# A fused attention and low-rank mixer kernel: the mixer of batches 2 to 8 in strips of 32 columns and rows, and a first batch in another order

## The chip, the cores and the metric

One core of a Trainium2 chip runs the whole kernel. The metric is the device time of one execution in microseconds, as the median of repeated runs; the results also hold one profiled execution with its trace. The engines are TensorE (PE, matmuls; PEld is its weight load), VectorE (DVE), ScalarE (ACT), GpSimd (POOL) and SyncE (SP, which issues most transfers).

## The reference

Eight batches of attention with normed queries and keys, 12 heads, 448 tokens, head size 64; the result goes through a low-rank mixer over tokens and a two-layer network over channels.

```python
def _attn_ref(q, k, v, g_q, g_k):
    def rmsnorm(x, g):
        rms = np.sqrt(np.mean(x * x, axis=-1, keepdims=True) + 1e-06)
        return x / rms * g
    q_n, k_n = (rmsnorm(q, g_q), rmsnorm(k, g_k))
    scores = scale * np.matmul(q_n, k_n.transpose(0, 1, 3, 2))
    ...
    return np.matmul(attn, v)          # softmax of the scores

def _moe_ref(x, U, V, w_ch1, w_ch2):   # x: (8, 448, 768), rank of U and V: 32
    xt = x.transpose(0, 2, 1)
    h = xt @ U @ V
    u = x + h.transpose(0, 2, 1)
    ch = np.maximum(u @ w_ch1, 0.0) @ w_ch2
    return u + ch
```

## The kernel before

The order of the work on every engine is written out by hand. In the code the eight batches are numbered 0 to 7, so that batches 2 to 8 of the title are `b` = 1 to 7. Each batch has 12 heads in six pairs and three groups of four heads; a group's q, k and v are loaded together (`load`), squared (`squares`), summed on VectorE (`sums`), turned into inverse roots on ScalarE (`roots`, lines 165 to 171), scaled (`scale`, line 173) and transposed (`turn`, then `take_q` and `take_k`, lines 349 to 373; from group 6 on by transfers, `turn_dma`). `values` copies v on GpSimd.

For a pair, scores go to PSUM and through the exponential on ScalarE into `E`: in batches 0 and 1 by rows of 128 keys (`Sc`, line 403), later as a whole pair (`Spair`, line 421), of which each takes the two double-bank score buffers of the pool `ps_sc`. `V` (line 450) multiplies `E` with the values, one half of the tokens at a time, and VectorE divides into `x`.

The mixer of one batch follows when `x` is complete. For `b` >= 1: `mix_t` (line 480) forms x^T U for six blocks of 128 channels, 24 matmuls with blocks of x as weights and 32 columns of U moving. VectorE casts the result (line 487), `mix_tr` (line 491) turns it in two transposes, and `mix_rows` (line 530) multiplies it with `Vm`, a copy of V that has zeros outside 32 rows for each of four positions: 24 matmuls of 128 columns in eight pieces. VectorE adds x (line 546), and SP issues four transposing transfers into `uT` (line 552). Batch 0 uses `mix_t0`, `mix` and `mix_rows` with `tz` instead.

The network is `up` (line 554, six matmuls of 448 columns for each of 24 blocks, ReLU on ScalarE mostly) and `down` (line 598, parts of six matmuls of 384 columns, four parts to an output half). A list `mlp` holds these pieces, and the mixer of batch b + 1 is put among the `down` parts of batch b (`pre`, `PRE`, lines 770 to 795). A list `att` holds the attention of the later batches. The loop from line 884 on interleaves both by costs in microseconds and by a model of how far each engine is (`at`, `runs`, `ready`): a `Spair` isn't put directly behind a mixer piece, and loads are held back (`later`, `turning`) while a mixer's transposes are queued on SP.

The first batch has no network beside it. Its order stands in the dict `extra` (line 651), whose entry `(i, r)` is put behind the scores of row block r of pair i, and in the lines from 799 on. `keep_busy` runs matmuls of the identity whose result nobody reads. GpSimd also issues the loads of the two weight matrices (`weights`: four pieces of `w1b`, eight of `w2b`).

Of the kernel before, what the change touches and what calls it, by code (L numbers as in the profile page):

```python
# [9 lines left out]
FP32 = mybir.dt.float32  # L10
# [16 lines left out]
def kernel(  # L27
# [19 lines left out]
    P = 128  # L47
# [199 lines left out]
    for va, vl in zip(va_bufs, vl_bufs):  # L247
        nc.vector.memset(va[:, :, D:D1], 1.0)
        nc.vector.memset(vl, 0.0)
        for e in range(2):  # L250
            nc.vector.memset(vl[e * R:(e + 1) * R, :, e * D1 + D:(e + 1) * D1], 1.0)
    for t, eng in zip(kT_bufs, (nc.vector, nc.gpsimd)):
        eng.memset(t[D:P, :, SM:S], 0.0)
        eng.memset(t[0:D, :, S:], 0.0)
# [54 lines left out]
    Vm = consts.tile([P, NQ, S + R], BF16)  # L309

    nc.gpsimd.memset(Vm, 0.0)

    def prep_v(lo, hi):
        for m in range(lo, hi):
            r = slice(m * rank, (m + 1) * rank)
            cols = Vf[r].rearrange("r (p j) -> r j p", j=NT)
            nc.gpsimd.tensor_copy(Vm[r, m, :SM].rearrange("r (t i p) -> r i t p", i=2, t=NJ),
                                  cols[:, :2 * NJ].rearrange("r (i t) p -> r i t p", i=2))
            nc.gpsimd.tensor_copy(Vm[r, m, SM:S], cols[:, 2 * NJ])
# [9 lines left out]
    tb_bufs = [consts.tile([P, 2 * P], BF16, name=f"tb{i}") for i in range(2)]  # L329
# [150 lines left out]
    def mix_t(b):  # L480

        pt = ps.tile([P, KD, rank], FP32, name="pu", tag="ps")
        for dt in range(KD):
            for j in range(NW):
                nc.tensor.matmul(pt[:, dt, :], xs[b][:, j, dt * P:(dt + 1) * P], Ub[:, j if j < NJ else NJ + b % 2, :],  # L485
                                 start=(j == 0), stop=(j == NW - 1))
        nc.vector.tensor_copy(tb_bufs[b % 2][:, :KD * rank], pt.rearrange("p k r -> p (k r)"))
        runs("pe", 0.62)
        runs("dve", 0.35)

    def mix_tr(b):
        pt = ps.tile([P, 2, P], BF16, name="pw", tag="ps")
        for i in range(2):
            nc.tensor.transpose(pt[:, i, :], tb_bufs[b % 2][:, i * P:(i + 1) * P], ident)
        tTs[b] = headp.tile([P, 2, P], BF16, name="tT", tag="tT")
        nc.vector.tensor_copy(tTs[b], pt)
        runs("pe", 0.11)
        runs("dve", 0.3)
# [11 lines left out]
    def mix(b, dt, scalar=False):  # L510
# [3 lines left out]
        nc.tensor.matmul(ph, tz[:, dt * P:(dt + 1) * P], Vm[:, 0, :S], start=True, stop=False)  # L514
# [15 lines left out]
    def mix_rows(b, w, half):  # L530

        odd = b % 2
        off = 0 if odd else 64
# [3 lines left out]
        if b < ROWS_FROM:  # L537
            nc.tensor.matmul(ph, Vm[:, 0, vc:vc + P], tz[:, h], start=True, stop=True)
        for i in range(HALF // P) if b >= ROWS_FROM else ():
            dt = half * (HALF // P) + i  # L540
            nc.tensor.matmul(ph[:, i * P:(i + 1) * P], Vm[:, dt % NQ, vc:vc + P], tTs[b][:, dt // NQ, :],  # L541
                             start=True, stop=True)
# [6 lines left out]
        if half == 1 and b >= ROWS_FROM:  # L549
            full = xs[b][:, w, :] if w < NJ else u_rest[lo:hi, :]  # L550
            c = off + w * P
            nc.sync.dma_start_transpose(uT[:, :, c:c + hi - lo], full)
# [95 lines left out]
    def turns(gi):  # L648
# [9 lines left out]
        (1, 2): [(0.4, turn, (1, 0)), (0, take_q, (1, 0)), (0, take_q, (1, 1)), (0, keep_busy, (8,))],  # L658
# [4 lines left out]
        (2, 3): [V2(1, 1), (0, prep_u, ())],  # L663
        (3, 0): [(0, keep_busy, (6,))],
        (3, 1): [V2(2, 0)],
        (3, 2): turns(2),
        (3, 3): [V2(2, 1), (0, take_k, (2, 1)), (0, squares, (3, 0, pool)), (0, values, (2,)), (0, load, (5,)),
                 (0, weights, (1,)), (0, prep_v, (0, 1)), (0, squares, (3, 1, pool)), (0, weights, (1,))],
        (4, 0): [V2(3, 0)],
        (4, 1): [V2(3, 1), (0, sums, (3, 0))],  # L670
        (5, 0): [(0.9, mix_t0, (0, 512))],
        (5, 1): [V2(4, 0)],
        (5, 2): [V2(4, 1), (0.39, mix, (0, 0))],
        (5, 3): [(0.39, mix, (0, 1)), (0.2, mix_t0, (512, 640)), (0, prep_v, (1, NQ)), (0, weights, (2,))],
# [95 lines left out]
    PRE = (14, 20)  # L770
    mlp = []
    for b in range(B):
# [8 lines left out]
        if ROWS_FROM <= nb < B:  # L781
            pre[n - PRE[nb > 1]] = [(0.77, mix_t, (nb,), nb)]
            pre[n - PRE[nb > 1] + 1] = [(0.11, mix_tr, (nb,), nb)]
            for piece in range(2 * NW):
                pre.setdefault(n - PRE[nb > 1] + 2 + (piece if nb > 1 else piece // 2), []).append(
                    (0.17, mix_rows, (nb, *divmod(piece, 2)), nb))
# [27 lines left out]
    for part in PARTS:  # L814
        scale_part(1, *part, nc.vector)
# [136 lines left out]
```

## Time and profile before

| | us |
|---|---|
| median of 3 runs (lowest, highest) | 582.67 (581.82, 583.47) |
| the profiled execution | 582.16 |
| its span | 580.3 |
| TensorE busy in the span | 570.9 |
| ScalarE, GpSimd, VectorE busy | 308.2, 210.2, 196.3 |

The span is that of the recorded instructions; the time has some 1.9 us around it. Busy time of TensorE counts a matmul to its modelled end, and neighbours overlap, so what a matmul costs is read from the distance between starts. The granted TensorE clock is 1.00 throughout. In a timeline a row gives start, duration, engine, line, operation, tiles and count, and in brackets how long the engine had been idle and what ended that.

### The profile page before, as it was taken

Reading aid. Unit: us, or ns where it says so; the run is one execution under the profiler, and the core shown is the slowest. Engines: PE = TensorE matmul, PEld = TensorE weight load, DVE = VectorE, ACT = ScalarE, POOL = GpSimd, SP = SyncE. Lnnn points to the kernel's source line nnn. Section 1 sums busy time; section 2 is a strip of 40 time slices with the busy share of each in tenths; the row PEclk is TensorE's granted clock in tenths of the full one; section 3 lists DMA queues with packets and bytes.
Section 4 is the critical chain, followed back from the end, with each engine's and each line's share of the span. In section 5 each row is a group of like instructions: output and inputs, shape, how many; then the busy total and the mean of one; then the engine's idle time right before and its main releaser. Section 6 shows DMA issues by size and latency. Waiting matters only on the chain.

```text
span 580.3 us, 11778 instructions
## 1 busy us (share of the span) xinstructions
PE 570.9 (98%) x4850; PEld 338.7 (58%) x4850; DVE 196.3 (34%) x459; ACT 308.2 (53%) x510; POOL 210.2 (36%) x310
## 2 busy tenths in 40 slices
PE   8899999999999999999999999999999999999997
PEld 7655556555665556655566555665556555655565
DVE  5676656212353232521244230542034210410011
ACT  6866660787445776277635568357752444014300
POOL 5995684265314514334514532441531000000000
PEclk9999999999999999999999999999999999999999
DMA  9899999683547642765247745366204210330022
GB/s 235 168 241 241 244 232 223 128 209 73 135 79 170 156 106 35 175 179 130 36 123 116 179 104 122 80 159 150 36 16 102 49 28 1 54 76 1 1 55 55
DMA packets 104829, 68.21 MB, mean 118 GB/s; under 512 B 66632, under 2 KB 101704, under 8 KB 104776
## 3 DMA queue, kind: packets, MB, share of 16 engines
q1 hardware_dynamic: 95124, 57.83, 43.2%
q0 software_dynamic: 9408, 9.44, 9.7%
q8 instruction: 38, 0.62, 0.5%
q10 hardware_dynamic: 244, 0.20, 0.1%
q14 instruction: 15, 0.12, 0.1%
HBM read 52.20 MB, written 11.01 MB: 109 GB/s over the span
## 4 chain that ended last, share of the span: by engine, by line
PE 92%; ACT 2%; DMA 1%; POOL 1%; DVE 1%; issue 1%; SPq 0%; POOLq 0%; ACTq 0%
PE ph L558 36%; PE po L605 36%; PE pv L466 6%; PE sc L436 2%; PE pv L462 2%; PE sl L427 2%; PE sl L438 2%; PE pm L541 2%; PE po L592 1%; ACT E L416 1%; PE sc L415 1%; DMA qT<-qn 1%; PE pu L485 1%; DMA qf<-in_q_dram 1%; PE pt L354 1%
## 5 line engine op out<-in xcount | busy, mean ns | idle before, releaser
L605 PE MATMUL po<-w2b,hT 128*128 128x384 bf16 x1296 | 229.6, 326 | 0.0
L558 PE MATMUL ph<-uT,w1b 128*128 128x448 bf16 x1140 | 228.7, 352 | 0.0
L605 PEld LDWEIGHTS <-hT 128*128 128x128 bf16 x1296 | 122.1, 98 | 71.8
L558 PEld LDWEIGHTS <-w1b 128*128 128x128 bf16 x1140 | 108.3, 98 | 93.7 <-issue 0.7
L565 ACT ACTIVATE hT<-ph 128x448 bf16<-128x448 f32 x184 | 98.2, 551 | 116.6 <-PE ph L558 115.2
L429 ACT ACTIVATE E<-sl,gg 128x448 bf16<-128x448 f32 x72 | 41.6, 630 | 71.7 <-PE sl L427 71.7
L193 POOL TENSOR_TENSOR qn<-qf,rs 128x384 bf16<-128x384 f32 x36 | 29.9, 830 | 137.5 <-ACT rs L170 126.8
L386 POOL TENSOR_SCALAR qT<-qT,gg 128x448 bf16<-128x448 bf16 x36 | 50.5, 1403 | 73.6 <-DMA qT<-qn 63.5
L469 DVE RECIPROCAL r<-pv 128x4 f32<-128x4 f32 x96 | 17.5, 182 | 173.0 <-PE pv L466 172.8
L441 ACT ACTIVATE E<-sc,gg 128x896 bf16<-128x896 f32 x72 | 69.0, 1024 | 0.0
L615 DVE TENSOR_TENSOR ob<-po,x 128x384 f32<-128x384 f32 x46 | 25.7, 558 | 99.8 <-PE po L605 97.6
L466 PE MATMUL pv<-va,E 128*128 128x65 bf16 x1152 | 57.1, 194 | 0.0
L466 PEld LDWEIGHTS <-E 128*128 128x128 bf16 x1152 | 50.5, 98 | 6.3
L162 DVE TENSOR_REDUCE ssq<-sq 128x14 f32<-128x896 f32 x45 | 46.8, 1078 | 2.4 <-ACT sq L140 2.3
L462 PE MATMUL pv<-vl,E 128*128 128x130 bf16 x192 | 42.2, 220 | 0.3 <-ACT E L416 0.2
L470 DVE TENSOR_TENSOR x<-pv,r 128x256 bf16<-128x256 f32 x96 | 40.7, 424 | 3.3
L416 ACT ACTIVATE E<-sc,gg 128x896 bf16<-128x896 f32 (+1 forms) x42 | 37.5, 951 | 3.5 <-PE sc L415 3.3
L546 DVE TENSOR_TENSOR x<-pm,x 128x384 bf16<-128x384 f32 x48 | 26.1, 552 | 11.3 <-PE pm L541 9.1
L193 POOL TENSOR_TENSOR kp<-kf,rs 128x384 bf16<-128x384 f32 x36 | 29.9, 830 | 0.0
L169 ACT ACTIVATE rs<-ssq,eps 128x28 f32<-128x28 f32 (+1 forms) x25 | 7.9, 314 | 38.0 <-DVE ssq L162 33.7
L462 PEld LDWEIGHTS <-E 128*128 128x128 bf16 x192 | 18.7, 97 | 9.7 <-issue 2.0
L439 ACT ACTIVATE E<-sl,gg 128x448 bf16<-128x448 f32 x36 | 23.0, 638 | 0.0
(105 smaller groups left out, 401.0 us busy)
## 6 DMA issues: line engine op xcount, KB each, us to landing
qf<-in_q_dram SPq DMA_DIRECT2D x23, 448.0 KB, 3.8
kf<-in_k_dram SPq DMA_DIRECT2D x23, 448.0 KB, 5.3
vf<-in_v_dram SPq DMA_DIRECT2D x48, 192.0 KB, 5.3
out_dram<-ob SPq DMA_DIRECT2D x48, 192.0 KB, 2.8
w1b<-in_moe_w_ch_dram POOLq DMA_DIRECT2D x4, 1152.0 KB, 19.8
w2b<-in_moe_w_ch_dram POOLq DMA_DIRECT2D x8, 576.0 KB, 18.0
vf<-in_v_dram SPq DMA_DIRECT2D x48, 32.0 KB, 5.1
out_dram<-ob SPq DMA_DIRECT2D x13, 96.0 KB, 3.4
```

The costliest lines, as they stand in the source:

```text
L162: nc.vector.tensor_reduce(ssqs[gi][:, i, :], sqs.pop((gi, i)), AX, ALU.add)
L193: nc.gpsimd.tensor_tensor(main.rearrange("p (t i) d -> p i t d", i=2), src[:, c, :2 * NJ].rearrange("p (i t) d -> p i t d", i=2), rs[:, c, ...
L386: nc.gpsimd.tensor_scalar(qT[:, a], qT[:, a], gg[:, 0:1], None, ALU.mult)
L416: nc.scalar.activation(es[(b, pr)][:, 2 * r:2 * r + n, :], sc[:, :n, :S], AF.Exp, scale=scal, bias=bias)
L429: nc.scalar.activation(E[:, 4 + i, :], ts[i], AF.Exp, scale=scal, bias=bias)
L441: nc.scalar.activation(E[:, 2 * r:2 * r + 2, :], tiles[r][:, :, :S], AF.Exp, scale=scal, bias=bias)
L462: nc.tensor.matmul(pv[:, i].rearrange("p e d -> p (e d)"), E[:, 2 * NJ, w:w + P], vl[:, lp, :], start=True, stop=False)
L466: nc.tensor.matmul(pv[:, i, e, :], E[:, 2 * j + e, w:w + P], va[:, (first_h + step * e) * NJ + j, :], start=False, stop=(e == 1 and j == N ...
L470: nc.vector.tensor_tensor(xs[b].rearrange("p i (h d) -> p i h d", d=D)[:, 2 * half:2 * half + 2, h0:h0 + step + 1:step, :], pv[:, :, :, :D ...
L558: nc.tensor.matmul(ph, w1b[:, dt, ht * P:(ht + 1) * P], uT[:, dt, off:off + S], start=(dt == 0), stop=(dt == KD - 1))
L565: nc.scalar.activation(hT[:, ht, off:off + S], ph, AF.Relu)
L605: nc.tensor.matmul(po, hT[:, ht, col:col + P], w2b[:, ht, half * HALF:(half + 1) * HALF], start=(ht == 0), stop=(ht == KH - 1))
```

## The change

Mixer, `b` >= 1. `mix_t` now has U as weights, 32 columns of them, and 192 columns of x moving; four such strips g = 0 to 3 write to PSUM partitions 32g to 32g + 31, so that the result comes out with 32 ranks times four channel quarters on the partitions and is cast once. There are 16 matmuls. `mix_tr` and its copy are gone. `mix_two` takes two row blocks w at once: for each, four matmuls with 32 rows of `Vr` (V copied four times down the partitions, without zeros) as weights and 32 rows of the cast as moving data, 192 columns each, into four banks: both buffers of `ps_sc`. The additions and the transposes into `uT` stand in `mix_two`. In `mlp` it stands at `PRE` + 2 and + `GAP`. Before a `mix_two` the planner takes one `down` of the batch before while its model of ScalarE or VectorE is behind TensorE.

First batch. The squares of group 1's q go from ScalarE to GpSimd and those of group 2's k from GpSimd to ScalarE, those of group 1's k behind the first exponential; `scales(2)` moves from behind (2, 1) to behind (2, 0), `values(1)` from (1, 3) to behind these scales; `V2(0, 1)`, the turns of group 2, `V2(2, 0)` and the mixer of batch 0 get other places; `gg` is copied between the two parts of the key's scaling. `keep_busy(10)` goes and another takes 8 instead of 14. The constants of the third value buffer and the second key buffer, which VectorE and GpSimd filled at the start, are filled by GpSimd later (`fill_mixer`); the fills of `Vm` and `tb` go, and `prep_v` is one pass instead of four.

```diff
-    Vm = consts.tile([P, NQ, S + R], BF16)
-    nc.gpsimd.memset(Vm, 0.0)
+    Vr = consts.tile([P, S + R], BF16)
+    nc.vector.memset(Vr[:, S:], 0.0)
...
     def fill_mixer():
         nc.gpsimd.memset(Uz, 0.0)
-        for t in tb_bufs:
-            nc.gpsimd.memset(t, 0.0)
+        fill_values(2, nc.gpsimd)
+        fill_keys(1, nc.gpsimd)
...
-        pt = ps.tile([P, KD, rank], FP32, name="pu", tag="ps")
-        for dt in range(KD):
-            for j in range(NW):
-                nc.tensor.matmul(pt[:, dt, :], xs[b][:, j, dt * P:(dt + 1) * P], Ub[:, j if j < NJ else NJ + b % 2, :],
-                                 start=(j == 0), stop=(j == NW - 1))
-        nc.vector.tensor_copy(tb_bufs[b % 2][:, :KD * rank], pt.rearrange("p k r -> p (k r)"))
+        pt = ps.tile([P, QC], FP32, name="pu", tag="ps")
+        for j in range(NW):
+            for g in range(NQ):
+                nc.tensor.matmul(pt[g * rank:(g + 1) * rank, :], Ub[:, j if j < NJ else NJ + b % 2, :],
+                                 xs[b][:, j, g * QC:(g + 1) * QC], start=(j == 0), stop=(j == NW - 1))
+        tTs[b] = headp.tile([P, QC], BF16, name="tT", tag="tT")
+        nc.vector.tensor_copy(tTs[b], pt)
...
-    def mix_tr(b):
...
+    def mix_two(b, ws):
+        odd = b % 2
+        off = 0 if odd else 64
+        ts = [ps_sc.tile([P, 2, 512], FP32, name="sc", tag="sc") for _ in range(2)]
+        for i, w in enumerate(ws):
+            vc = w * P if w < NJ else (SM if odd else S - P)
+            for g in range(NQ):
+                r = slice(g * rank, (g + 1) * rank)
+                nc.tensor.matmul(ts[g // 2][:, g % 2, i * QC:(i + 1) * QC], Vr[r, vc:vc + P], tTs[b][r], start=True, stop=True)
+        runs("pe", 0.4)
+        for i, w in enumerate(ws):
...
+                nc.vector.tensor_tensor(full[:, h].rearrange("p (g c) -> p g c", g=2),
+                                        ts[half][lo:hi, :, i * QC:(i + 1) * QC],
+                                        xs[b][lo:hi, w, h].rearrange("p (g c) -> p g c", g=2), ALU.add)
+                runs("dve", 0.56)
+            c = off + w * P
+            nc.sync.dma_start_transpose(uT[:, :, c:c + hi - lo], full)
...
-        (0, 0): [(0, keep_busy, (8,))],
+        (0, 0): [(0, squares, (1, 1)), (0, take_k, (0, 1)), (0, sums, (1, 1)), (0, sums, (2, 0)), (0, keep_busy, (8,))],
...
-        (0, 2): scales(1) + [(0, squares, (2, 1, pool)), (0, keep_busy, (8,))],
+        (0, 2): scales(1) + [(0, weights, (1,)), (0, keep_busy, (8,))],
...
-        (1, 1): [V2(0, 0), (0, keep_busy, (6,))],
...
-        (1, 3): [(0.4, turn, (1, 1)), (0, take_k, (1, 0)), V2(0, 1), (0, take_k, (1, 1)), (0, sums, (2, 1)),
-                 (0, values, (1,)), (0, load, (4,)), (0, weights, (1,))],
-        (2, 1): scales(2) + [(0, weights, (1,)), V2(1, 0)],
+        (1, 1): [(0, squares, (2, 1)), V2(0, 0), (0, keep_busy, (6,))],
...
+        (1, 3): [(0.4, turn, (1, 1)), (0, take_k, (1, 0)), (0, sums, (2, 1)), (0, take_k, (1, 1)), (0, keep_busy, (4,))],
+        (2, 0): scales(2) + [(0, values, (1,)), (0, load, (4,)), (0, weights, (1,))],
+        (2, 1): [V2(1, 0)],
...
-        (3, 1): [V2(2, 0)],
-        (3, 2): turns(2),
...
+        (3, 1): [(0.4, turn, (2, 0)), (0, take_q, (2, 0)), (0, take_q, (2, 1))],
+        (3, 2): [(0.4, turn, (2, 1)), (0, take_k, (2, 0)), V2(2, 0)],
...
-        (5, 0): [(0.9, mix_t0, (0, 512))],
+        (5, 0): [(0, sums, (3, 0)), (0.45, mix_t0, (0, 256))],
...
+            at_ = n - PRE[nb > 1]
+            pre[at_] = [(0.6, mix_t, (nb,), nb)]
+            pre[at_ + 2] = [(0.4, mix_two, (nb, (0, 1)), nb)]
+            pre[at_ + GAP[nb > 1]] = [(0.4, mix_two, (nb, (2, 3)), nb)]
...
-    keep_busy(10)
-    for part in PARTS:
-        scale_part(1, *part, nc.vector)
+    scale_part(1, *PARTS[0], nc.vector)
     nc.vector.tensor_copy(gg, pg)
-    squares(1, 0)
+    scale_part(1, *PARTS[1], nc.vector)
     fill_mixer()
+    squares(1, 0, nc.gpsimd)
+    turn(0, 0)
+    keep_busy(8)
+    take_q(0, 0, True)
+    take_q(0, 1, True)
+    turn(0, 1)
+    keep_busy(14)
+    take_k(0, 0)
+    sums(1, 0)
...
+            if after_pair and mixes(f) or f is mix_two and max(at["act"], at["dve"]) > at["pe"]:
+                e = next((i for i in range(im, len(mlp)) if mlp[i][1] is down), None)
+                if e is not None and mlp[e][3] < mlp[im][3]:
+                    mlp.insert(im, mlp.pop(e))
```

Of batch 0's mixer only the places change: `mix_t0` of the first 512 channels is split in two and `mix(0, 0)` moves behind the last scores. The rest of the diff removes `squares(1, 1)`, `sums` and `take_k(0, 1)` from where they stood ahead of the loop, since they are in `extra` now, and adapts line by line to the new names.

More of the change, by code (lines that the diff above doesn't have):

```diff
@@ L513, in mix @@
         xb = xs[b][:, :, dt * P:(dt + 1) * P]
-        nc.tensor.matmul(ph, tz[:, dt * P:(dt + 1) * P], Vm[:, 0, :S], start=True, stop=False)
+        nc.tensor.matmul(ph, tz[:, dt * P:(dt + 1) * P], Vr[:, :S], start=True, stop=False)
         for j in range(NJ):
@@ L536, in mix_rows @@
         vc = w * P if w < NJ else (SM if odd else S - P)
[L537 to L542, printed above, removed]
+        nc.tensor.matmul(ph, Vr[:, vc:vc + P], tz[:, h], start=True, stop=True)
         x = xs[b][:, w, h]
@@ L548, in mix_rows @@
         runs("dve", 0.56)
[L549 to L552, printed above, removed]
     def up(b, ht):
@@ L821 @@
     values(0)
-    turn(0, 0)
-    keep_busy(14)
-    take_q(0, 0, True)
-    take_q(0, 1, True)
-    squares(1, 1)
-    turn(0, 1)
-    take_k(0, 0)
-    sums(1, 0)
-    sums(1, 1)
-    take_k(0, 1)
-    sums(2, 0)
     stage_tiles(3)
@@ L865, in mixes @@
     def mixes(f):
-        return f in (mix_t, mix_tr, mix_rows)
+        return f in (mix_t, mix_two)
     def ready(f, a):
@@ L875, in ready @@
         if f is sums and a[0] > DMA_FROM:
-            return not any(m[1] in (mix_t, mix_tr) for m in mlp[max(0, im - 1):im + 3])
+            return not any(m[1] is mix_t for m in mlp[max(0, im - 1):im + 3])
         if ca >= a_one:
@@ L918 @@
             f(*a)
-            turning = f is mix_t and a[0] > 0 or turning and a != (a[0], NW - 1, 1)
+            turning = f is mix_t or turning and not (f is mix_two and a[1][1] == NW - 1)
             cm += c
```

76 lines of the change are left out of this document (32 added, 44 removed).

## The prediction

> **What bounds the kernel now.** I read the page first, then the stretches by engine, then two engines' timelines. The first line is engine busy time; the digits are the busy tenths of 40 equal slices; the last two are stretches: busy time of each engine, granted clock, DMA share, GB/s.
>
> ```profile
> PE 570.9 (98%) x4850; PEld 338.7 (58%) x4850; DVE 196.3 (34%) x459; ACT 308.2 (53%) x510; POOL 210.2 (36%) x310
> ...
> PE   8899999999999999999999999999999999999997
> ...
> 0.00:41.00 41.00, 35.41 (x473) 26.55 (x474) 27.45 (x85) 30.48 (x47) 33.65 (x51) 1.00 0.95 213
> 41.00:580.00 539.00, 535.45 (x4379) 312.11 (x4377) 168.90 (x375) 277.69 (x464) 176.54 (x260) 1.00 0.50 110
> ```
>
> From 41 us to the end TensorE is the bound: it stands still for 3.6 of 539 us. There only less TensorE time counts, and any new wait of TensorE counts in full. Before 41 us TensorE partly runs filler (`keep_busy`), and ScalarE's exponentials of batch 0 set the pace. So I split the time into the head, to the last exponential of batch 0 at 35.5 us, and the chain of TensorE work behind it: a shift of the head moves the end by as much.
>
> The mixer of one batch on TensorE (start, duration, shape, count; an instruction's step is the next start minus its own, since durations overlap):
>
> ```profile
> 92.32 0.75 PE L485 MATMUL pu<-Ub,x 128*128 128x32 bf16 x24
> 92.92 1.14 PE L605 MATMUL po<-w2b,hT 128*128 128x384 bf16 x6
> 93.89 0.28 PE L494 MATMUL pw<-ident,tb 128*128 128x128 bf16 x2
> 94.01 1.14 PE L605 MATMUL po<-w2b,hT 128*128 128x384 bf16 x6
> 94.98 0.50 PE L541 MATMUL pm<-tT,Vm 128*128 128x128 bf16 x6
> 95.32 1.14 PE L605 MATMUL po<-w2b,hT 128*128 128x384 bf16 x6
> ...
> 106.16 0.36 PE L427 MATMUL sl<-qT,kT 64*128 64x448 bf16 x2
> 106.36 0.54 PE L436 MATMUL sc<-qT,kT 64*128 64x448 bf16 x4
> 106.83 0.36 PE L438 MATMUL sl<-qT,kT 128*128 128x448 bf16 x1
> ```
>
> `mix_t` steps 92.92 - 92.32 = 0.60, `mix_tr` 0.12, six `pm` 0.34, so 24 of them 1.36: 2.08 us a batch. The last lines show part-array matmuls, 64 rows each: two of 448 columns step 0.20 together, as long as one full-array one (six `ph` of 448 take 1.14, 0.19 each). So two row halves run side by side. Four step 0.47, two rounds of 0.187 plus 0.10: going into or out of the part-array form costs about 0.095 each way (the same on entry: 24 `po` of 0.1625 from 102.17 end at 106.07, `sl` starts at 106.16).
>
> The head, ScalarE and GpSimd:
>
> ```profile
> 12.10 2.80 ACT L416 ACTIVATE E<-sc,gg 128x896 bf16<-128x896 f32 x3
> 14.78 0.33 ACT L169 ACTIVATE rs<-ssq,eps 128x28 f32<-128x28 f32 x1
> ...
> 20.37 1.91 ACT L416 ACTIVATE E<-sc,gg 128x896 bf16<-128x896 f32 x2 [1.04 <-PE sc L415]
> 22.53 0.32 ACT L169 ACTIVATE rs<-ssq,eps 128x28 f32<-128x28 f32 x1 [0.26 <-DVE ssq L162]
> ...
> 28.27 4.33 ACT L416 ACTIVATE E<-sc,gg 128x896 bf16<-128x896 f32 x5 [0.21 <-PE sc L415]
> ```
>
> ```profile
> 12.13 1.68 POOL L143 TENSOR_TENSOR uT<-qf 128x896 f32<-128x896 f32 x1 [2.15 <-DMA qf<-in_q_dram]
> ...
> 20.41 0.82 POOL L201 CAST va<-vf 128x768 bf16<-128x768 f32 x1
> ...
> 23.25 1.68 POOL L174 TENSOR_TENSOR qn<-qf,rs 128x896 bf16<-128x896 f32 x1 [0.43 <-issue]
> ```
>
> ScalarE runs from 12.10 to 35.50 with only some 2 us of waits, most of it the 1.04 before group 1's first scores.
>
> **The mixer, seven times.** New `mix_t`: 16 matmuls of 192 columns, in four rounds of four column strips. A full-array matmul of 192 columns would step 0.083 (between `pm`, 0.34/6 = 0.057 at 128, and `po`, 0.1625 at 384). No row shows column strips, nor four parts at once. Bounds: side by side, 4 x 0.083 + 0.19 for entry and exit = 0.52; one after another, 16 x 0.083 + 0.19 = 1.52. I take the first, since the nearest row, the 64-row pair, is wholly side by side. `mix_tr` is gone. New `mix_two`: two rounds of four 32-row strips, 2 x 0.083 + 0.19 = 0.36, twice: 0.71 (one after another, 0.85 each). Sum 1.23 against 2.08: 0.85 x 7 = **-5.9 us**.
>
> VectorE gets the same 16 halves of additions over 384 columns (0.55 each), one 192-column cast as before (0.36), and loses a 0.29 copy; it is off the path. The four uT transposes per batch stay on SP's queue; the second pair now lies behind fewer `down` parts. The tightest case is the step into batch 3, where six parts and two V halves, 6.7 us, remain between the last `mix_two` and the first `up`. The additions take 2.2, two transposes queue at 1.25 each, the last lands 2.5 after issue: about 5.7. Hidden, with 1 us to spare; if two output issues (0.6 each) stand ahead, nothing is left.
>
> **A new wait.** `mix_two` takes both double-bank score buffers that `Spair` uses. TensorE must wait there for the exponentials, and all `down` matmuls behind it wait too. From the start of a `Spair` to its last exponential, rows of batch 4 give 3.9 us (305.91 to 309.79). In the new order three of the 14 `mix_two` stand 0.87 + 3 x 0.975 = 3.8 us behind it and the rest more; a modelled delay of ScalarE is ahead of that. In turn a `Spair` stands two `down` parts behind a `mix_two` once, 2.5 us until its first use against four additions and a latency, 2.8. Together 4 x 0.1 to 0.2: **+0.5**; bounds 0 and 3 (squares of 1.9 us on ScalarE in front of one `Spair` in two).
>
> **The head.** `keep_busy(10)` goes and `gg` moves ahead of the second key part: q's copy starts about 0.5 sooner. Keys still need the second part: VectorE ends it at 10.2 instead of 10.03, but the transposes no longer stand behind 14 fillers: they start at 10.25 instead of 10.63, so the first exponential comes at 11.8 instead of 12.10. Behind it ScalarE has now the squares of group 1 (0.84, before they filled the wait for scores) and later those of group 2's keys (0.84, from GpSimd). So the roots of group 1 start at 11.8 + 4 x 0.93 - 0.1 = 15.35 instead of 14.78, its keys are ready 0.5 later, scores of pair 2 likewise (20.9 against 20.37), the old 1.04 wait being filled by the moved squares. Group 2's roots start at 20.9 + 0.93 = 21.85 instead of 22.53: 0.7 won. But `values(1)` has moved behind both group 2 scales on GpSimd. It is done 0.72 + 3.35 + 1.41 = 5.5 after the roots (scale and copy rows above), where it was ready at 21.8 before. `V2(2,0)` needs it and stands on TensorE ahead of the last scores of pair 3. ScalarE wants those 0.5 + 0.93 x 5 + 0.6 = 5.75 after the roots; TensorE gives them at 5.55 + 0.48 (V) + 0.4 = 6.4. So a new wait of 0.7, and 0.2 more at pair 4, whose first exponential moves from 28.27 to about 29.0. Behind it splitting `mix_t0` saves about 0.2. **+0.6**, bounds -0.6 (ScalarE without any wait, 11.8 + 6 x 3.4 + 1.0 + 1.7 = 34.9) and +1.2.
>
> Off the path: GpSimd's fills (about 0.95, by the 0.20 and 0.28 fills of that engine) and q's squares of group 1 (1.68) end by 12.1, in its 2.15 wait for qf. The mask Vm's fill and its 3.45 us of copies at 36 to 39 vanish, so the first w2b issue moves from 39.3 to about 36.5. w1b's second piece goes from 26.5 to 27.3; it lands 20 us on, near 47, and is first read near 50.
>
> Sum: the profiled execution took 582.16 (span 580.3 and 1.9 around it). -5.9 + 0.5 + 0.6 = -4.8 gives 577.4; the three runs' median, 582.67, lies 0.5 higher, so 577.9. I predict **577.6**, between.
>
> **Rivals.** (1) Weight loads show. A strip's reload may not hide behind the matmuls of the same rows. For it: column strips all use all rows, and the first load after a change of form costs 0.095. Against it: in the four `sc` matmuls the second pair reloads the same rows and nothing shows. Three more rounds at 0.095 in `mix_t`: +0.29 x 7 = 2.0, so 579.6.
>
> The Trainium skill, TensorE: Matmul & The Clock Gate, Part 3 (The mechanism), says that a weight load overlaps running matmuls only when the row group differs, which is this rival; the `sc` row, where it did not differ, disagrees for row strips.
>
> (2) The other side: column strips run one after another. Each strip needs its own stream of x over all 128 rows, where row halves share one; no row here excludes it. `mix_t` is then 1.52: +7.0, so **584.6**, slower than before. It decides from a step of 0.064 per strip matmul (0.021 in my case, 0.083 here): 4.8/7/16 = 0.043 more eats the gain.
>
> The Trainium skill, TensorE: Matmul & The Clock Gate, Part 3 (Measured speedup vs the span model), gives 2.38 times for three column strips; that speaks against this rival, and no run here shows it yet.
>
> (3) Score buffers bind: `mix_two` waits at most places instead of three, about 0.25 x 14 = 3.5 in place of 0.5: 580.6. Against it: most places have 4.2 us or more.
>
> (4) w1b's second piece comes late. It is issued 0.8 later, and with w2b's pieces asked for 2.8 earlier, more share the queues. If it took 24 us to land instead of the median 20, `up` would wait about 2 us near 50 us: 579.6. Against it: issues of w2b start behind all of w1b.
>
> **Chances.** Forecast 0.66, (1) 0.13, (3) 0.07, (2) 0.08, (4) 0.06. What this kernel's measurement tells from no change is 0.3%, 1.75 us, so faster means under 580.9. Faster: 0.66 + 0.13 + 0.05 of (3) and (4), = 0.84; the other 0.08 of these two is no change, and (2) is slower, 0.08. Range 575.8 (head at its lower bound, no stalls: 582.16 - 5.9 - 0.6) to 580.5 (loads shown, stalls 1, head 1.0: -5.9 + 2.0 + 1.0 + 1.0 + 0.3).
>
> **What would show it.** Right: `mix_t` steps about 0.52, each `mix_two` about 0.36, `pw` gone, TensorE's waits for ScalarE or VectorE under 1 us after 41 us; pair 4's first exponential near 29. Wrong: `mix_t` near 0.8 (rival 1) or 1.5 (rival 2); rows of TensorE waiting for E or uT after 41 us (rival 3 or late transposes); no new wait in front of pair 3's last scores, with the head then shorter by up to 0.6.

## The result, and the profile after

The changed kernel took 578.57 us, the median of five runs (577.25 to 579.88), against 582.17 (581.82 to 583.47) for five runs of the kernel before on the same chip: a ratio of 0.9932, 95% interval 0.9918 to 0.9946, or 3.1 to 4.8 us. The profiled execution of the changed kernel took 578.57, its span 576.8, 3.5 less than before.

The lines of the page that answer to those shown of before, engine busy time and TensorE's busy tenths:

```profile
PE 565.8 (98%) x4728; PEld 326.7 (57%) x4728; DVE 193.7 (34%) x450; ACT 307.1 (53%) x510; POOL 205.7 (36%) x305
...
PE   8889999999999999999999999999999999999997
```

The two stretches of the changed kernel (length, busy time of PE, PEld, DVE, ACT, POOL with counts, granted clock, DMA share, GB/s):

```profile
0.00:41.00 41.00, 34.24 (x472) 26.28 (x473) 25.78 (x82) 30.07 (x46) 28.50 (x45) 1.00 0.97 213
41.00:580.00 539.00, 531.54 (x4258) 300.46 (x4256) 167.87 (x369) 276.99 (x465) 177.23 (x260) 1.00 0.51 110
```

TensorE is still the bound behind 41 us. A fixed mark divides the time better than 41 us: the first full `up` matmul (the first row of `ph<-uT,w1b`), which started at 41.14 before and at 42.37 after. From there to TensorE's end it was 535.72 before and 531.01 after: 4.71 less. The head is 1.23 longer. 4.71 - 1.23 = 3.5, the difference of the spans. The two rows, before and after:

```profile
41.14 1.30 PE L558 MATMUL ph<-uT,w1b 128*128 128x448 bf16 x6
...
42.37 1.30 PE L567 MATMUL ph<-uT,w1b 128*128 128x448 bf16 x6
```

**Where the 4.71 came from.** Steps (next start minus own) of each line, summed from that mark on; the first two columns are before and after:

| | before | after | difference |
|---|---|---|---|
| the mixer's own matmuls | 14.38 (9.37 + 4.23 + 0.78) | 7.09 (3.13 `mix_t`, 3.96 `mix_two`) | -7.29 |
| `down`, L605 and L614 | 213.15 | 215.22 | +2.07 |
| score matmuls of `Spair`, L436 and L440 | 17.08 | 17.82 | +0.74 |
| everything else | 291.11 | 290.88 | -0.23 |

`down` has not changed; its 2.07 are, but for 0.1, the entries into the part-array form, 21 of them at 0.094, since the step of the last `down` matmul ahead of a strip is 0.256 in place of 0.162. With the 2.07 put to its account the mixer went from 14.38 to 9.16, from 2.05 to 1.31 a batch. In the timeline of TensorE in the changed kernel (start, duration, line, shape, count, idle time before and its releaser):

```profile
93.64 0.51 PE L489 MATMUL pu<-x,Ub 128*32 128x192 bf16 x16
94.09 3.10 PE L614 MATMUL po<-w2b,hT 128*128 128x384 bf16 x18
97.12 0.34 PE L505 MATMUL sc<-tT,Vr 32*128 32x192 bf16 x8
97.40 4.07 PE L614 MATMUL po<-w2b,hT 128*128 128x384 bf16 x24
101.40 0.34 PE L505 MATMUL sc<-tT,Vr 32*128 32x192 bf16 x8
101.68 2.12 PE L614 MATMUL po<-w2b,hT 128*128 128x384 bf16 x12
103.74 0.36 PE L431 MATMUL sl<-qT,kT 64*128 64x448 bf16 x2
...
106.65 0.36 PE L431 MATMUL sl<-qT,kT 64*128 64x448 bf16 x2
106.85 0.35 PE L440 MATMUL sc<-qT,kT 64*128 64x448 bf16 x2
107.67 0.37 PE L440 MATMUL sc<-qT,kT 64*128 64x448 bf16 x2 [0.46 <-ACT E L445]
107.96 0.36 PE L442 MATMUL sl<-qT,kT 128*128 128x448 bf16 x1
```

Sixteen `mix_t` matmuls step 94.09 - 93.64 = 0.45, a `mix_two` 0.28; with 0.09 for the entry 0.54 and about 0.38. The only idle time that is named in these rows is that of the last score matmuls. Nothing waits at a `mix_two`. But the first `Spair` of two now stands behind both `mix_two` and two `down` parts more, at 103.74, 2.9 us before the second, where before they stood at 101.29 and 106.16, 4.9 apart. By the code that is the planner's rule, which keeps a `Spair` off the place right behind a mixer piece; no run changes that rule. The second `Spair` then wants score buffers whose exponentials aren't done: the first one's end at 107.62. The first `Spair` before, and the exponentials of the changed kernel:

```profile
101.29 0.36 PE L427 MATMUL sl<-qT,kT 64*128 64x448 bf16 x2
...
105.70 1.92 ACT L445 ACTIVATE E<-sc,gg 128x896 bf16<-128x896 f32 x2
```

From the first of these score matmuls to the row behind them it takes 107.96 - 106.85 = 1.11 us instead of the usual 0.47. So this one `Spair` costs 0.64, more than the 0.46 of named idle time, which counts only from the modelled end of the matmul before.

**Where the 1.23 went.** ScalarE of the changed kernel, batch 0:

```profile
11.05 1.01 ACT L420 ACTIVATE E<-sc,gg 128x896 bf16<-128x896 f32 x1 [0.72 <-PE sc L419]
...
20.16 1.01 ACT L420 ACTIVATE E<-sc,gg 128x896 bf16<-128x896 f32 x1 [0.42 <-PE sc L419]
21.09 0.32 ACT L169 ACTIVATE rs<-ssq,eps 128x28 f32<-128x28 f32 x1
...
27.42 0.64 ACT L420 ACTIVATE E<-sc,gg 128x448 bf16<-128x448 f32 x1 [0.71 <-PE sc L419]
28.27 6.86 ACT L420 ACTIVATE E<-sc,gg 128x896 bf16<-128x896 f32 x8 [0.21 <-PE sc L419]
38.43 0.97 ACT L538 CAST uT<-ph 128x448 bf16<-128x448 f32 x2 [3.30 <-PE ph L536]
```

The last exponential ends at 35.13, which is 0.4 earlier than before (35.51). But the first squares had started 0.58 earlier in this execution too, because the first load landed sooner; counted from the first squares the exponentials end 0.2 later. What is new is the time from the last exponential to the first full `up`: 7.24 against 5.63, 1.6 more. The chain of waits of the changed kernel (start, length, what) tells why:

```profile
20.08 11.90 DMA qf<-in_q_dram
32.02 0.10 issue
32.12 1.68 POOL sq L143
33.83 1.09 DVE ssq L162
34.92 0.33 DVE x L527
...
35.81 0.34 PE ph L533
```

The q of group 3 was issued at 20.08 and took 11.9 us. GpSimd's squares of it started at 32.12 (28.34 before). VectorE stood in front of `sums(3, 0)` for 3.48 us, and behind it in its queue were a mixer cast and the last divisions of batch 0, for which TensorE's `mix(0, 0)` waited 1.34. The wait on each, in the changed kernel:

```profile
33.83 1.09 DVE L162 TENSOR_REDUCE ssq<-sq 128x14 f32<-128x896 f32 x1 [3.48 <-POOL sq L143]
...
35.80 0.35 PE L533 MATMUL ph<-Vr,x 128*128 128x448 bf16 x1 [1.34 <-DVE x L474]
```

GpSimd of the changed kernel shows what changed ahead of that load:

```profile
18.56 1.05 POOL L285 DMA_DIRECT2D w1b<-in_moe_w_ch_dram  x1
...
32.12 1.67 POOL L143 TENSOR_TENSOR sq<-qf 128x896 f32<-128x896 f32 x1 [2.72 <-DMA qf<-in_q_dram]
```

The first piece of w1b (1152 KB) is now issued 1.5 us ahead of q; before it was issued at 21.76, 1.2 behind it (20.55). GpSimd before:

```profile
21.76 1.05 POOL L278 DMA_DIRECT2D w1b<-in_moe_w_ch_dram  x1
...
28.34 1.67 POOL L143 TENSOR_TENSOR sq<-qf 128x896 f32<-128x896 f32 x1 [0.36 <-DMA qf<-in_q_dram]
```

The DMA view of the stretch 24 to 26 us of the changed kernel, queue by queue (packets, MB, time as a share of 16 engines; q0 carries GpSimd's loads, q1 those of SP):

```profile
q0 software_dynamic: 200, 0.31, 91.0%
q1 hardware_dynamic: 152, 0.08, 27.1%
```

The same stretch and view of the kernel before:

```profile
q1 hardware_dynamic: 291, 0.36, 108.5%
```

While w1b is under way, SP's queue gets 0.08 MB in 2 us in place of 0.36. In the kernel before, GpSimd's queue moved nothing yet in that stretch: the packets of w1b began to run behind 26 us.

### The profile page after: what moved, and what is told of

It is laid out like the page before. It is cut to its first block, busy times and chain, and to the rows that moved or that the text cites. A ratio compares the mean times of both kernels' runs of the same rounds, so it can differ in the third digit from the quotient of the medians.

```text
span 576.8 us, 11533 instructions
## 1 busy us (share of the span) xinstructions
PE 565.8 (98%) x4728; PEld 326.7 (57%) x4728; DVE 193.7 (34%) x450; ACT 307.1 (53%) x510; POOL 205.7 (36%) x305
## 4 chain that ended last, share of the span: by engine, by line
PE 92%; DMA 3%; SPq 2%; ACT 1%; DVE 0%; issue 0%; POOL 0%; POOLq 0%
PE ph L567 37%; PE po L614 36%; PE pv L470 6%; PE sc L440 2%; DMA qf<-in_q_dram 2%; PE pv L466 2%; PE sl L431 2%; PE sl L442 2%; PE po L601 1%; DMA vf<-in_v_dram 1%; PE sc L505 1%; PE sc L419 1%; PE pu L489 1%; PE pt L358 0%; SPq L115 0%; SPq L110 0%
## 5 line engine op out<-in xcount | busy, mean ns | idle before, releaser
L614 PE MATMUL po<-w2b,hT 128*128 128x384 bf16 x1296 | 223.8, 326 | 0.0
L614 PEld LDWEIGHTS <-hT 128*128 128x128 bf16 x1296 | 123.0, 98 | 78.9 <-issue 2.5
L512 DVE TENSOR_TENSOR x<-sc,x 128x384 bf16<-128x384 f32 x42 | 20.8, 551 | 15.7 <-PE sc L505 15.7
```

The lines of the kernel that those rows point to most:

```text
L614: nc.tensor.matmul(po, hT[:, ht, col:col + P], w2b[:, ht, half * HALF:(half + 1) * HALF], start=(ht == 0), stop=(ht == KH - 1))
```

## The experiments

Two theories stood at the start. First: the mixer's strips run side by side and bring the whole gain; second: w1b's first piece delays group 3's q, and this costs about 1 us of the head. Rivals are in the expectations. "Gap" is the time from the last exponential of batch 0 to the first full `up`; times are medians, ratios against the kernel before on the same chip.

| | squares of q 3 | gap | first full `up` | to the end | time | ratio (95%) |
|---|---|---|---|---|---|---|
| before | 28.34 | 5.63 | 41.14 | 535.72 | 582.17 | |
| after | 32.12 | 7.24 | 42.37 | 531.01 | 578.57 | 0.9932 (0.9918 to 0.9946) |
| a0_changed | 32.30 | 6.99 | 42.54 | 531.01 | 578.68 | 0.9934 (0.9913 to 0.9954) |
| e1_old_head | 29.12 | 5.63 | 41.24 | 531.35 | 577.88 | 0.9915 (0.9900 to 0.9929) |
| e2_sums_late | 33.15 | 8.25 | 44.11 | 531.01 | 578.75 | 0.9934 (0.9918 to 0.9951) |
| e10_late_q_borne | 33.45 | 6.44 | 43.26 | 531.01 | 578.76 | 0.9927 (0.9911 to 0.9943) |
| e4_q_first | 32.82 | 6.11 | 43.90 | 531.02 | 578.46 | 0.9926 (0.9911 to 0.9941) |
| e5_values_early | 29.41 | 5.72 | 40.38 | 531.01 | 578.02 | 0.9915 (0.9897 to 0.9933) |
| e3b_w1b_later | 30.87 | 6.22 | 42.85 | 530.97 | 579.03 | one run |
| e9_values_w1b_later | 29.14 | 7.09 | 42.45 | 530.98 | 578.89 | 0.9937 (0.9924 to 0.9950) |
| e14_values_spaced | 30.70 | 6.26 | 40.93 | 531.68 | 578.58 | 0.9942 (0.9920 to 0.9963) |
| e7_strips_in_turn | 33.19 | 7.23 | 43.43 | 531.22 | 578.76 | 0.9922 (0.9902 to 0.9943) |
| e13_one_strip | 32.81 | 7.65 | 43.05 | 536.11 | 583.98 | 1.0031 (1.0010 to 1.0051) |

From the mark to the end the traces agree to 0.01 us where the code there is the same, so differences of a few tenths count in that column. The head's columns come from one execution each, and loads land differently from one to the next: the four executions with the changed kernel's first batch (after, a0, e7, e13) have their first full `up` at 42.4 to 43.4, the two with the old one at 41.1 and 41.2. The times of one kernel spread over 2 us, so they don't separate heads that differ by 1 us.

Two things in these traces tie the late head to q. The load took 9.5 to 11.9 us in the eight executions that issued w1b's first piece ahead of it and left q's place alone, and 7.6 to 8.7 in the four that issued w1b behind it (before, e1, e3b, e9). And in the five executions that have the changed kernel's order behind these squares and in which TensorE waited at `mix(0, 0)` for VectorE (after, a0, e7, e13, e14), the first full `up` came 10.24 to 10.25 us behind the start of q's squares, whether these began at 30.70 or at 33.19: there q's landing sets the first `up`.

**Is the loss in the head?** a0_changed is the changed kernel once more.

> The changed kernel as it is, as the base for the others on the same chip: 0.993 of the time before. The first up matmul comes 1.2 us later than in the kernel before (42.4 against 41.1), and from there to the end it takes 4.7 us less. If the late first up was a chance of that one execution (transfers land differently each time), it should now lie near 41.2 or 41.7, as the head was forecast.

The late first `up` came again (42.54), with q's squares at 32.30. e1_old_head has the new mixer with the old order of the first batch, of which two places are shown:

```diff
-        (0, 2): scales(1) + [(0, weights, (1,)), (0, keep_busy, (8,))],
+        (0, 2): scales(1) + [(0, squares, (2, 1, pool)), (0, keep_busy, (8,))],
...
-        (2, 0): scales(2) + [(0, values, (1,)), (0, load, (4,)), (0, weights, (1,))],
...
+        (1, 3): [(0.4, turn, (1, 1)), (0, take_k, (1, 0)), V2(0, 1), (0, take_k, (1, 1)), (0, sums, (2, 1)),
+                 (0, values, (1,)), (0, load, (4,)), (0, weights, (1,))],
+        (2, 1): scales(2) + [(0, weights, (1,)), V2(1, 0)],
```

> The new mixer with the first batch in the old order (except that V is copied once, and the mask is not filled). Theory: the mixer gains 5.2 by its steps less 0.5 to 0.7 of a new wait, and the new order of the first batch loses about 1.2. Then this kernel is 4.5 to 5 below the time before (ratio 0.9915 to 0.9925) and 1 us faster than the changed kernel, with the first up at 41.1. Rival: the head is worth nothing or gains, as its first exponential comes sooner; then this kernel is no faster than the changed one (ratio 0.993 or above).

Its gap is 5.63, that of before, its first `up` 41.24, and its time 577.88: the mixer alone brings all of the gain, and the new order of the first batch costs about 1.2 us at the first `up` by the traces (0.3 of that is lost again behind the mark, where e1 takes 531.35). By the times it is not told apart (0.9900 to 0.9929 against 0.9913 to 0.9954 on the same chip).

**Is it VectorE's place behind the late q?** e2_sums_late takes `sums(3, 0)` out of the way of the mixer and of the divisions.

```diff
-        (5, 0): [(0, sums, (3, 0)), (0.45, mix_t0, (0, 256))],
+        (5, 0): [(0.45, mix_t0, (0, 256))],
...
-        (5, 3): [(0.39, mix, (0, 0)), (0.39, mix, (0, 1)), (0.2, mix_t0, (512, 640)), (0, weights, (2,))],
+        (5, 3): [(0.39, mix, (0, 0)), (0.39, mix, (0, 1)), (0.2, mix_t0, (512, 640)), (0, sums, (3, 0)), (0, weights, (2,))],
```

> Only the first sum of group 3 moves on VectorE, from ahead of the first mix_t0 to behind the third. Theory: in the changed kernel VectorE stood 3.5 us at this sum, which waits for GpSimd's squares and these for q's transfer, and with it the cast of mix_t0, the divisions of V and so mix(0, 0) on TensorE (1.3 us). Without that the wait is gone and the first up comes about 1.2 us sooner, ratio 0.991. Rival: the head is set by ScalarE's exponentials, which end later by the squares and the wait for values(1); then the wait goes elsewhere and the first up stays within 0.3 of 42.4.

A miss. VectorE's wait was gone, and TensorE waited at the same place for another. A row of TensorE in e2_sums_late:

```profile
36.83 0.35 PE L533 MATMUL ph<-Vr,x 128*128 128x448 bf16 x1 [1.64 <-POOL Vr L325]
```

GpSimd makes `Vr` (`prep_v`) behind the squares of the same late q: a second queue stands behind that load. e10_late_q_borne keeps the edit of e2 and moves `prep_v` ahead of these squares as well.

```diff
-        ... (0, prep_u, ()), (0, squares, (3, 0, pool)),
-                 (0, weights, (1,)), (0, prep_v, ()), (0, squares, (3, 1, pool)), (0, weights, (1,))],
+        ... (0, prep_u, ()), (0, prep_v, ()), (0, squares, (3, 0, pool)),
+                 (0, weights, (1,)), (0, squares, (3, 1, pool)), (0, weights, (1,))],
```

> q of group 3 stays late, but nothing of batch 0 stands behind it: on GpSimd the copy of V goes ahead of its squares, on VectorE its sum goes behind the third mix_t0. Theory: the late q hurts only by what queues behind it in order, on VectorE the cast of mix_t0 and V's divisions, on GpSimd the copy of V that mix(0, 0) needs (the last run showed this second one by a 1.6 us wait). Then TensorE's wait of 1.1 to 1.6 at mix(0, 0) is gone and the first up comes 1.0 to 1.3 sooner (41.2 to 41.5 with exponentials ending at 35.3). Rival: the sums of group 3 then come too late for the roots and turn of group 3, and TensorE waits at that turn for what it won.

With q at its latest of all (33.45) the gap is 6.44, 0.6 to 1.2 under that of the changed kernel: neither wait is left. The first `up` still came at 43.26, since ScalarE had lost 1.7 us earlier in that execution (the roots of group 2 at 22.77 in place of 21.09, behind late scores). The time did not move. So the two queues are shown, and their price is 0.6 to 1.2 us by the gap.

**Can the load be brought forward?** e4_q_first issues group 3's q ahead of U, V and group 2's values.

```diff
+    load_qk(3, 0)
     load_u()
     load_v(2)
-    load_qk(3, 0)
```

> Only the load of group 3's q moves on SP's queue, ahead of the loads of U, V and group 2's values. Theory: in the changed kernel it was issued at 20.1, 1.5 us behind the first weight piece (1152 KB), and landed 12 us later at 32.0; issued near 14 it lands before 24, the squares start when GpSimd is free, near 29.5 instead of 32.1, the sum is done by 32.2 instead of 34.9, and the first up comes 1 to 1.3 us sooner (ratio 0.991). Rival: transfers issued in between only change places, group 2's values or U come late instead, and the first up stays at 42.4.

q landed 3.8 us after its issue at 15.09, and nothing was won. Group 2's values were late instead. A row of GpSimd in e4_q_first:

```profile
31.93 0.30 POOL L203 CAST vl<-vf 64x128 bf16<-64x128 f32 x1 [1.50 <-DMA vf<-in_v_dram]
```

And one of TensorE, which waited for U's copy behind them in GpSimd's queue:

```profile
32.91 0.61 PE L523 MATMUL pu<-x 128*128 128x256 bf16 x4 [0.90 <-POOL x L333]
```

The engines of the DMA are full from 20 us on (their share is 1.14 to 1.17 in 20 to 32 us of the changed kernel), and the transfers trade places. The same with w1b: e3_w1b_later issues its first piece between the scalings of group 2.

```diff
-        (0, 2): scales(1) + [(0, weights, (1,)), (0, keep_busy, (8,))],
+        (0, 2): scales(1) + [(0, keep_busy, (8,))],
...
-        (2, 0): scales(2) + [(0, values, (1,)), (0, load, (4,)), (0, weights, (1,))],
+        (2, 0): scales(2)[:2] + [(0, weights, (1,))] + scales(2)[2:] + [(0, values, (1,)), (0, load, (4,)), (0, weights, (1,))],
```

> Only the first piece of w1b moves on GpSimd's queue, from behind group 1's scaling (issued at 18.6 to 19.3) to between the two scalings of group 2 (near 23.5). Theory: that piece, asked for 1.5 us ahead of group 3's q, takes the transfer engines' time and makes q land 11.9 us after its issue; before the change q was issued 1.2 us ahead of the piece and landed after 7.7. With the piece later, q lands near 28 and the squares of group 3 start by 30 instead of 32.1 to 33.2; the first up then comes 0.8 to 1.5 sooner than in the changed kernel (42.4 to 42.5), unless the keys of group 2, 1.05 later on GpSimd, eat it: they show as a longer wait for the scores of pair 4. Rival: q is late because of group 2's values or U and V that stand ahead of it on SP's queue; then the squares stay at 32.

It took 579.45 (median), a ratio of 0.9938 (0.9924 to 0.9953): nothing won. e3b_w1b_later is the same kernel, run for its trace.

> The changed kernel with w1b's first piece issued between the two scalings of group 2 in place of behind those of group 1; it is run for its trace. Theory (the first piece's packets take the DMA engines from group 3's q): q lands within 8.5 us of its issue in place of 11.9, GpSimd's squares of it start at 28.5 to 29.5 in place of 32.1 to 33.2, and the first up matmul comes at about 41.3 in place of 42.4 to 43.4. Rival (another transfer is then late, as when q was loaded first): q early, but TensorE's first up no sooner than 42.3, with a wait named for GpSimd's values or casts.

Half right. q no longer held GpSimd up (its squares began at 30.87, straight behind other work), so w1b's first piece did delay it. But the first full `up` came at 42.85: TensorE waited 0.78 for group 1's values, 0.9 for group 2's scaled keys behind w1b's issue, and 0.39 for w1b itself. With e5_values_early only the values move:

```diff
-        (2, 0): scales(2) + [(0, values, (1,)), (0, load, (4,)), (0, weights, (1,))],
+        (2, 0): [(0, values, (1,))] + scales(2) + [(0, load, (4,)), (0, weights, (1,))],
```

> Only values(1) moves back ahead of the scalings of group 2, into the 2.2 us in which GpSimd stands still. The forecast's step on it: TensorE's wait for vl (0.6) and ScalarE's wait ahead of pair 3's last exponential (0.71) go, and the exponentials end 0.7 to 0.9 sooner, at 34.3 to 34.7. Theory of the late q: the first up stays within 0.3 of 42.4 all the same, as the sum on VectorE holds it. Rival: the exponentials set the head, and the first up moves 0.7 or more.

Two rows of ScalarE in e5_values_early: the wait of 0.71 ahead of pair 3's last exponential is gone, and pair 4 starts at 27.80.

```profile
21.90 5.68 ACT L420 ACTIVATE E<-sc,gg 128x896 bf16<-128x896 f32 x7
27.80 6.86 ACT L420 ACTIVATE E<-sc,gg 128x896 bf16<-128x896 f32 x8 [0.21 <-PE sc L419]
```

Its exponentials end at 34.66, its first `up` is at 40.38, the earliest of all, where the late-q theory had it within 0.3 of 42.4. But q landed at 29.27 here, in time, so this execution had no late q to show. The edit doesn't guarantee that: e14_values_spaced, with the same first batch, waited for q until 30.70 and had its first `up` at 40.93. In both w1b's first piece is issued at 18.9, ahead of q as in the changed kernel, and q still took less time (9.5 and 10.2 us) than in the six others with that order (11.3 to 11.9); why is not shown. e9_values_w1b_later does both:

```diff
...
+        (2, 0): [(0, values, (1,))] + scales(2)[:2] + [(0, weights, (1,))] + scales(2)[2:] + [(0, load, (4,)), (0, weights, (1,))],
```

> Both repairs of the first batch: values of group 1 ahead of the scalings of group 2, and w1b's first piece between those scalings. Theory (the two losses add: the wait of 0.7 for the values, and q's late landing): first up at about 40 us, as early as or earlier than with the values alone (40.4), and about 0.990 of the kernel before. Rival (transfers trade places, the values' move has already taken all there is): 40.4 to 41.3, and 0.9915 as with the values alone.

The two repairs don't add, and 42.45 is later than theory and rival had it. q is early (29.14) and TensorE's wait for the values is gone, but it waits 0.9 for group 2's scaled keys, which now stand behind w1b's issue, so that ScalarE loses 0.83 where the changed kernel lost 0.71 and the exponentials end at 35.36. And w1b, issued at 23.54 instead of 18.56, isn't there when the first part of `up` of batch 0 wants it. A row of TensorE in e9_values_w1b_later:

```profile
38.70 0.74 PE L585 MATMUL sc<-uT,w1b 128*128 128x448 bf16 x3 [1.25 <-DMA w1b<-in_moe_w_ch_dram]
```

So w1b's first piece is hemmed in from both sides: issued at 18.6 it holds up q (by 1 us only, and at no cost to the first `up`, in e5), at 23.5 it is itself late. The kernel before issued it at 21.76 and had neither wait.

**Do the strips run side by side, and does their order matter?** e7_strips_in_turn walks strip by strip in `mix_t`.

```diff
-        for j in range(NW):
-            for g in range(NQ):
+        for g in range(NQ):
+            for j in range(NW):
```

> In mix_t the loops over strips and row blocks change places: the four matmuls of one strip follow each other, as many and as large as before. If the strips run side by side (theory), 13 instead of 4 of the 192-column streams follow one another: a mix_t steps about 13 x 0.083 + 0.1 = 1.2 instead of 0.45, and the time rises by 7 x 0.73 = 5.1, to the time before the change or a little below (ratio 0.998 to 1.003). If the matmuls of a strip form ran at their rate for another reason (short loads of 32 columns, say), the order would change nothing.

A miss: the 16 matmuls step 0.48 in place of 0.45, where the theory had 1.2, and the stretch to the end takes 531.22, 0.2 more instead of 5.1. The order hardly matters, as its rival said. A row of TensorE in e7_strips_in_turn:

```profile
94.71 0.54 PE L489 MATMUL pu<-x,Ub 128*32 128x192 bf16 x16
```

In the trace the starts lie at 0, 13, 27, 40 ns, then at 93, 107, 120, 133, and so on, rounds 82 ns apart. In the changed kernel a round's four starts are 3.3 ns apart. 13 ns is four times 3.3: the first matmul of the second strip starts after four have been handed out, without waiting until the first strip is through its four. So, as the starts read, each strip takes its own matmuls in turn, past those that stand ahead of it for another strip (a record doesn't name its strip). The theory's mistake would then be the order of the starts, not the work side by side. e13_one_strip separates that from the rival, under which a strip matmul is cheap wherever it goes. From the second row block on one strip takes all twelve matmuls, and the other three get nothing behind their first:

```diff
-                nc.tensor.matmul(pt[g * rank:(g + 1) * rank, :], Ub[:, j if j < NJ else NJ + b % 2, :],
+                r = 0 if j else g
+                nc.tensor.matmul(pt[r * rank:(r + 1) * rank, :], Ub[:, j if j < NJ else NJ + b % 2, :],
...
```

> The changed kernel with 12 of the 16 matmuls of mix_t (those of windows 2 to 4) sent to one and the same column strip, so the three other strips stay as they are after the first round and the mixer's result for batches 2 to 8 is not the reference's. Theory (strips run side by side, each taking its own matmuls in turn): one strip now has 13 matmuls in turn, 13 x 0.0825 + 0.19 = 1.26 us a batch in place of 0.54; 7 x 0.72 = +5.0, so the stretch from the first up matmul to the end goes from 531.0 to about 536.0 us and the time to about 583.7. Rival (a strip matmul is cheap wherever it goes, and the short steps come from its 32 columns of weights): no change, 531.0 and about 578.7.

As the theory had it: 536.11 from the mark to the end (536.0 expected), 583.98 in time (583.7). A row of TensorE in e13_one_strip; sixteen take 95.50 - 94.32 = 1.18 up to the next `down`:

```profile
94.32 1.25 PE L490 MATMUL pu<-x,Ub 128*32 128x192 bf16 x16
```

In its trace the four first starts are 3.3 ns apart and the twelve others 82.5 ns each. So the rival is out: four column strips do four times the work of one in the same time.

**The added wait at a `Spair`.** e14_values_spaced is e5 with a stricter planner:

```diff
-            return at["dve"] <= at["pe"] + 0.3 and at["act"] <= at["pe"] + 1.0
+            return at["dve"] <= at["pe"] + 0.3 and at["act"] <= at["pe"] + 0.5
```

> Values of group 1 ahead of the scalings of group 2, and the planner lets a Spair out only when its modelled ScalarE is at most 0.5 us behind TensorE (1.0 in the changed kernel), which moves some Spair back by one down or up part. Theory (the added wait comes from a Spair two parts behind another): the wait of 0.46 us at the score matmuls is gone, these steps fall from 17.8 to about 17.2 us, and the stretch from the first up to the end from 531.0 to about 530.4; about 0.990 of the kernel before. Rival (score buffers are short anyway): the wait turns up at another Spair or at a mix_two, and the stretch stays at 531.0.

The score matmuls' steps fell to 17.07, the figure of before, so the cause of that wait, a `Spair` too close behind another, is shown. But the stretch grew to 531.68. Rows of TensorE in e14_values_spaced:

```profile
106.39 0.54 PE L440 MATMUL sc<-qT,kT 64*128 64x448 bf16 x4
...
184.89 1.29 PE L567 MATMUL ph<-uT,w1b 128*128 128x448 bf16 x6 [1.33 <-DVE ob L624]
```

And one of SP's queue in the same kernel:

```profile
182.42 1.21 SPq L517 DMA_TRANSPOSE uT<-u_rest  x1
```

This is the step into batch 3. The VectorE operation named had ended at 184.16, 0.7 us earlier, so it isn't what was waited for. The last transpose into `uT` was issued at 182.42 behind two transposes of q and k and takes 2.4 to land (the median of that stretch): 184.8, when TensorE went on. In the changed kernel it is issued at 181.09 and `up` starts at 185.51. 0.75 was won and 1.33 lost.

No version was shown to beat the changed kernel. The lowest medians, 577.88 and 578.02, are those of the new mixer with the old first batch and of the early values; their intervals overlap with the changed kernel's.

## Why the prediction was right, and where it was not

Forecast 577.6, measured 578.57: inside the range, on the side forecast, and 1.0 above the point. The terms, in the profiled execution:

| term | forecast | measured |
|---|---|---|
| mixer, seven times | -5.9 | -5.2 |
| added wait | +0.5 | +0.74 |
| head | +0.6 | +1.2 |
| rest | 0 | -0.2 |
| sum | -4.8 | -3.5 |

- **The mixer.** The mechanism held: strips side by side, form changes at 0.094 in and 0.091 to 0.097 out (0.095 forecast). `mix_t` was 0.54 (0.52 forecast), a `mix_two` 0.38 (0.36), so a batch 1.31 in place of 1.23, and the old mixer 2.05 in place of 2.08. These two make the 0.7: 7 x 0.11.
- **Rival 1, weight loads show, and rival 2, column strips in turn.** Neither. e13's strip takes one matmul after another through all 128 rows at 82.5 ns, what 192 columns cost by the estimate from full-array rows (0.083), with a new weight load for each. The Trainium skill, TensorE: Matmul & The Clock Gate, Part 3 (The mechanism), lets a load overlap only when the row group differs; here it never differed, and nothing showed. The same section of the Trainium skill has matmuls start strictly in program order; e7's starts, 13 ns apart across strips whose own matmuls take 82.5 each, don't fit that for column strips. Within the run of rounds this case has four for four; with the form changes a whole `mix_t` has 16 x 0.0825 / 0.54 = 2.4 times.
- **The added wait.** The price was near, the place wrong. Forecast was a `mix_two` behind a `Spair` in three places and one `Spair` behind a `mix_two`. No `mix_two` waited (rival 3 didn't come), and 0.64 of the 0.74 is one `Spair` behind another at 106.85 (another, at 352.62, has 0.12). The forecast had left out that the planner moves `Spair` off the place behind a `mix_two`.
- **The head, up to pair 4.** Right: the roots of group 2, and the wait of 0.7 for the values, came as written (0.71 at 27.42). Counted from the first squares, the first exponential came 0.47 sooner (0.3 forecast) and pair 4's first 0.58 later (0.73 forecast).
- **The head, behind the exponentials: the step that failed.** "Behind it splitting `mix_t0` saves about 0.2." In truth this part grew by 1.6, of which e1 undoes all. So the premise that a shift of the last exponential moves the end by as much didn't hold either: that exponential came 0.38 earlier, and the first `up` 1.23 later. The working followed w1b's second piece, issued later, and not its first, issued 3.2 us earlier and now ahead of q. Its bounds (-0.6 to +1.2) came from ScalarE alone, and +1.23 lies just outside; in three more executions of the same first batch the first `up` came 1.4 to 2.3 later than before. That the total lies in the range is owed to the mixer's term, which was near, and to the width of the range. The rows that would have told were there: 448 KB of q had taken 7.6 us with w1b issued behind it, and the DMA share of the stretch to 41 us was 0.95.
- **Off the path.** The transposes into batch 3 were hidden, as forecast; e14 shows that cover used up, at 1.3 us. The late second piece of w1b (rival 4) cost nothing: issued at 26.44, when 26.53 was the time before, it wasn't later at all.

## What to carry to other kernels

When an edit moves a bulk load, price it at the transfers it overtakes, not only at its own reader: find the small load issued next, and ask which engine queues stand behind that one. Where the engines of the DMA are full, moving loads about trades one wait for another, and the place has bounds on both sides. On TensorE, a product of rank 32 pays as four strips even when it is cut into short stretches, as long as one entry and exit (0.19 us here) is small against what it saves.

## What the hardware showed that was not expected

- Four column strips take their matmuls independently, and the order of issue hardly matters in the two orders tried: 0.48 strip by strip against 0.45 round by round for 16 matmuls of 192 columns. The Trainium skill, TensorEngine Tiling (Array Packing), Tiling Modes (Key Properties), says that tiles operate independently and that a change of mode drains the engine; the traces agree with both, the drain at 0.094 us on the way in and 0.091 to 0.097 on the way out.
- Two DMA queues share by packets, not by bytes. In 30 to 32 us of the kernel before the counts are 206 and 202, the bytes 0.32 and 0.15 MB. In 24 to 26 us of the changed kernel they are 200 and 152, and 0.31 and 0.08 MB, since a packet of w1b has 1.5 KB and one of SP's there 0.5 on average (104 of the 152 have 256 bytes). The Trainium skill, DMA: Bandwidth & Descriptors, Queues, rings and completion order, has each engine change between queues packet by packet, and the trace agrees. Next to a queue of large packets, one of small packets moves the fewer bytes.
